# The start of a spectral layer: rows rounded from the raw row, statistics reordered

## The chip, the core and the metric

The kernel runs on one core of a Trainium2 chip. A core has TensorE (PE in the profile, with its weight loads as PEld), VectorE (DVE), ScalarE (ACT), GpSimd (POOL) and SyncE (SP), which here only issues transfers. Each engine works through its own queue in order, and an instruction that waits holds up what stands behind it. The metric is the device time of one execution in microseconds, the median of several runs.

## The reference

Four layers are applied to a sequence of 2048 rows of 576 numbers, alternately a Fourier mixing layer (A) and a gated long convolution (B), each on the normalized row and added to its input:

```python
def _layernorm(x, axis=-1, eps=1e-5):
    m = jnp.mean(x, axis=axis, keepdims=True)
    v = jnp.var(x, axis=axis, keepdims=True)
    return (x - m) / jnp.sqrt(v + eps)
...
a = jnp.einsum("bsd,ed->bse", x, dft_hid_re)
b = jnp.einsum("bsd,ed->bse", x, dft_hid_im)
y = jnp.einsum("ts,bse->bte", dft_seq_re, a) - jnp.einsum("ts,bse->bte", dft_seq_im, b)
...
x = x + _A_ref(_layernorm(x, axis=-1), ...)
x = x + _B_ref(_layernorm(x, axis=-1), B_k, B_v, B_shift_k, B_ssm_k, B_ssm_D)
x = x + _A_ref(_layernorm(x, axis=-1), ...)
x = x + _B_ref(_layernorm(x, axis=-1), B_k, B_v, B_shift_k, B_ssm_k, B_ssm_D)
```

B multiplies q by a causal convolution along the sequence of (short convolution of k, times v) with the kernel ssm_k, to which ssm_D adds at position 0. q is the normalized row; k, v, ssm_k, ssm_D are inputs, so all of the convolution can be computed beside the first A layer.

## The kernel before

**Numbers in two halves.** A float32 operand of a matmul is cut into a high half (rounded to the type float32r) and a low half (the value less the high half). `split` (lines 98 to 100) does so: ACT writes the high half, DVE subtracts it and writes the low half. A product takes three matmuls: high by high, high by low and low by high.

**Layer 1.** The 2048 positions are held as 16 "rows" of 128 partitions by 576 (the name row means such a block below). The sequence transform comes first. `layer` runs over steps (g, tb, k): g is the real or imaginary part, tb one of four blocks of 512 outputs, k one of 16 rows. A step loads one tile of `c_mat` (128 x 512), splits it (`load_c`; its halves lie in `mats`, written by L99 and L100), and multiplies row k by it: 12 matmuls into the banks `s0` to `s3` and two into `rm`, 14 in all. Step 0 is row 0 with tile 0, step 1 row 1 with tile 1, and so on.

**Making a row ready.** `load_x` issues a row's load into `early`. `norm_stats` takes its statistics: two half-row statistics (L183) and their joining (L184) on DVE, eps added (L185, DVE), the power -0.5 on POOL (L186). `normed` then forms the bias on DVE (L192) and scales the row in place on ACT (L193). `to_x` rounds the scaled row into `xs`, a part of `mats` (L197, ACT), and writes its low half with two subtractions on DVE (L199, L200). `get_x0` does this for row j, loads row j + 2 and takes row j + 1's statistics ahead.

**The branch.** `branch` is a generator that runs layer 2's convolution beside layer 1, one piece at each `next(br)`. In its first stage it loads rows of `ssm_k` ("kernel rows") and `v` with constants `f1c`, splits them (`f1_split`, into `f1r`), multiplies them (`f1_products`, banks `bf`), evacuates them on ACT (L453) and stores them. The first kernel row is row 1, then row 0, to whose first partition `ssm_D` is added (L431, DVE). The first constant is loaded through SP and rounded on ACT (L418), the others come by POOL's queue.

**The order of the work.** Within each engine a planner draws the order when the program is built; it takes what it holds to be ready, by need. `tc.issue_after(i)`, and `behind(i, j, ...)` for several, force that what is traced in the block on `i`'s engine stands behind `i` on that engine's queue; on other engines they do nothing, and they bring no wait. Lists keep the instructions to refer to: `parted` (the last split of the branch), `rounded`, `scaled`, `biased`, `pows`, `made` (a row's last subtraction), `halved` (the last tile's split), `stored` (the last evacuation of the branch), `anchor` (loads of c_mat).

**The beginning** (lines 769 to 787): row 0's load, 14 matmuls on zeros (`warm`), the first loads of the branch, row 0 made ready, the tiles 0 and 1 loaded and split, the loads of rows 1 and 2, then row 1 and two pieces of the branch. Then `layer` takes over.

Of the kernel before, what the change touches and what calls it, by code (L numbers as in the profile page):

```python
# [12 lines left out]
AF = mybir.ActivationFunctionType  # L13
OP = mybir.AluOpType
# [12 lines left out]
ASTAT = 8  # L27
XLEAD = 3
WARM = 14
EARLY = 6  # L30
ROWS = (0, 1, 2, 3, 4, 5, 6, 7, 8, 9)
K_FIRST = 4
# [34 lines left out]
def fnet_h3_kernel(ctx: ExitStack, tc: tile.TileContext, x, c_mat, w_re, w_im, k_pad, v, shift_k,  # L67
# [94 lines left out]

    anchor, made, rounded, pows, biased, halved, added, evac, parted, stored = [], [], [], [], [], [], [], [], [], []

    scaled = []

    def load_after(dst, src):
        with tc.issue_after(anchor[-1]):
            return nc.sync.dma_start(dst, src).ins
# [9 lines left out]
    def norm_stats(src):  # L179
        m = ring["stat"]()  # L180
        st, mv, ve, rs = m[:, :12].rearrange("p (a c) -> p a c", a=2), m[:, 12:14], m[:, 14:15], m[:, 15:16]
        for i in range(2):
            nc.vector.bn_stats(st[:, i, :], src[:, i * HD:(i + 1) * HD])  # L183
        nc.vector.bn_aggr(mv, st)  # L184
        nc.vector.tensor_scalar(ve, mv[:, 1:2], EPS, None, op0=OP.add)  # L185
        pows.append(nc.gpsimd.tensor_tensor(rs, ve, mhalf, OP.pow).ins)  # L186
        return mv, rs, m[:, 16:17]

    def normed(src, y):
        mv, rs, nb = norm_stats(src)  # L190
        yield
        biased.append(nc.vector.tensor_scalar(nb, mv[:, 0:1], rs, -1.0, op0=OP.mult, op1=OP.mult).ins)  # L192
        scaled.append(nc.scalar.activation(y, src, AF.Identity, bias=nb, scale=rs).ins)  # L193

    def to_x(y, j):
        t = xs[:, j, :]
        rounded.append(nc.scalar.activation(t[:, :D], y, AF.Copy).ins)  # L197
        h = t.bitcast(F32)
        nc.vector.tensor_tensor(t[:, D:D + REM], y[:, NC * P:], h[:, NC * P:D], OP.subtract)  # L199
        made.append(nc.vector.tensor_tensor(t[:, D + REM:], y[:, :NC * P], h[:, :NC * P], OP.subtract).ins)  # L200
        return t
# [10 lines left out]
    X = [None] * J  # L212
    CT = {}

    def load_c(step):
        g, tb, k = step
        raw = ring["craw"]()
        anchor.append(load_after(raw, c_mat[g, tb, k]) if anchor else nc.sync.dma_start(raw, c_mat[g, tb, k]).ins)
        c = ring["cs"]()
        t = c[:, :NT], c[:, NT:]  # L220
        with behind(*stored):
            halved[:] = split(t[0], t[1], raw)
        CT[step] = t
# [127 lines left out]
    def branch():  # L351
# [55 lines left out]
        def f1_loads(upto):  # L407
            while loads[0] < min(upto, len(todo)):
                j, src = todo[loads[0]]
                loads[0] += 1  # L410
                if j not in fcs:
                    fcs[j] = two(ring["fc"]())
                    if pows:
                        load_fr(fcs[j], f1c[j])
                    else:
                        raw = two(tmp[:, :2 * P])
                        nc.sync.dma_start(raw, f1c[j])
                        nc.scalar.activation(fcs[j], raw, AF.Copy)  # L418
                landed[j, src] = ring["land"]()
                nc.sync.dma_start(landed[j, src], (ssm_k if src else v)[:, j, :])  # L420
                if src and j == 0:
                    nc.sync.dma_start(tmp[:1, D:], ssm_d[None, :])

        def f1_split(j, src):
            r = landed.pop((j, src))
            if not src:
                row = rows[j // 2][:, j % 2, :]
                nc.vector.tensor_tensor(row, row, r, OP.mult)
                r = row
            elif j == 0:  # L430
                nc.vector.tensor_tensor(r[:1], r[:1], tmp[:1, D:], OP.add)  # L431
            if j < K_FIRST:
                xf = parts("xf")
                parted[:] = split(xf[0], xf[1], r)
                return xf
            if not src:
                t = ring["xp"]()
                paired[:] = t[:, :2 * D], t[:, 2 * D:]
            h, l = (t.rearrange("p (a s d) -> p a s d", a=2, s=2)[:, :, src, :] for t in paired)
            parted[:] = split(h, l, two(r))  # L440
            return tuple(paired)
# [15 lines left out]
        def visit(half):  # L457
            if visits and visits[0][0] <= half:
                f1_products(*visits.pop(0)[1:])

        for n, (j, src) in enumerate(todo):
            f1_loads(n + 1)
            if n < 2:
                yield
            xf = f1_split(j, src)
            if j < K_FIRST:
                visits += [(2 * n + 2, j, fcs[j], xf, hf * HD, HD, "so", hf * D + src * HD) for hf in range(2)]
            elif src:
                visits += [(2 * n + 3, j, fcs[j], xf, at, VW, "sp", at) for at in range(0, 2 * D, VW)]
            if n:  # L470
                f1_loads(n + 3)
            later = [m for m in range(n + 1, len(todo)) if todo[m][1] == 0 and 7 * (todo[m][0] // 2 + 1) > made_ops]
            for half in range(2):
                visit(2 * n + half)
                if later and n > 2:
                    left = 7 * (todo[later[0]][0] // 2 + 1) - made_ops
                    for _ in range(-(-left // (2 * (later[0] - n) - half)) if left > 0 else 0):
                        next(conv)
                        made_ops += 1
                yield  # L480
# [204 lines left out]
    def normed_x(src, y, junk):  # L685
        sm, rs, nb = sums(src, junk)
        yield
        nc.vector.tensor_tensor(nb, sm, rs, OP.mult)
        nc.scalar.activation(y, src, AF.Identity, bias=nb, scale=rs)
# [3 lines left out]
    def load_x(j):  # L693
        if j < J:
            XL[j] = ring["x"]()
            nc.sync.dma_start(XL[j], x[:, j, :])

    def stats0(j):
        if j < J and j not in LN:
            src = XL.pop(j)  # L700
            LN[j] = src, normed_x(src, src, ring["junk"]()) if j >= ASTAT else normed(src, src)
            next(LN[j][1])

    def get_x0(j):
        if X[j] is None:
            if j > 0:
                load_x(j + 2)
            stats0(j)
            if j > 0:
                with behind(*stored):  # L710
                    stats0(j + 1)
            src, ln = LN[j]
            with behind(*rounded[-1:]):
                next(ln, 0)
            X[j] = to_x(src, j)

    def done0(j, xa):
        nc.sync.dma_start(xa_d[j], xa)
# [50 lines left out]
    load_x(0)  # L769
    warm()  # L770
    next(br)
    get_x0(0)
    with tc.issue_after(biased[0]):
        next(br)
        with behind(*parted, scaled[0]):
            load_c((0, 0, 0))
        load_x(1)
        with behind(rounded[0]):
            load_c((0, 0, 1))
        load_x(2)  # L780
    used = 4
    first_lo = parted[1]
    next(br)
    next(br)
    with behind(first_lo):
        get_x0(1)
    next(br)
    next(br)
    spent = passed = 0.0
    total = (I2_END + 1 - MID_FROM) * STEP + 3 * 2 * TB * PIECE  # L790
# [384 lines left out]
```

## Time and profile before

| | us |
|---|---|
| median of 3 runs | 1185.11 |
| lowest, highest | 1184.79, 1185.26 |
| the profiled execution's own time | 1183.61 |
| its span, first to last instruction | 1181.8 |
| PE idle before its first matmul | 1.52 |
| ACT busy from 15 to 60 | 40.82 of 45 |
| DVE busy from 15 to 60 | 39.65 of 45 |

The mean granted TensorE clock is 0.999 of full speed. In the page's first part a row gives each engine's busy time, its share of the span and its instructions. A row of the windows gives a stretch and its length, then busy time and number of instructions for PE, PEld, DVE, ACT and POOL, the granted clock, the share of DMA engines busy and GB/s. A row of the waits says who waited for whom: us in all, times, longest. A row of the timeline gives start and length in us, the engine, the line, the operation, what it writes and reads, the shape and the number of instructions merged into the row; in brackets the idle time of the engine before it and what ended that. Matmuls and the passes of ACT and DVE overlap a little with the next one, so a start may lie before the end of the one before.

### The profile page before, as it was taken

The numbers are of one execution on the slowest core, as the hardware profiler recorded it, in microseconds if no ns is written. First come the engines' busy times: TensorE is split into PE (matmuls) and PEld (weight loads), VectorE is DVE, ScalarE is ACT, GpSimd is POOL, SyncE is SP. The second block draws the span as 40 slices with busy tenths as digits, with TensorE's granted clock in tenths as the row PEclk, the third lists the DMA queues.
The fourth block names the chain that finished last, engine by engine and source line by source line (L and its number), as shares of the span: only waits on it lengthen the run. The fifth ranks groups of instructions, "written<-read, shape, count | busy, mean of one in ns | idle before, by whom it ended". The sixth has DMA issues, their size and how long they took to land.

```text
span 1181.8 us, 18082 instructions
## 1 busy us (share of the span) xinstructions
PE 1167.8 (99%) x6198; PEld 989.1 (84%) x6198; DVE 868.6 (73%) x1564; ACT 650.8 (55%) x1280; POOL 75.5 (6%) x115
## 2 busy tenths in 40 slices
PE   8999999999999999999999999999999999999997
PEld 6776667988888888888888898888888888889997
DVE  7899983788877778787756765865776777774764
ACT  8865655577766667766645666534444445550210
POOL 2310000000000000001101111000000000001111
PEclk9999999999999999999999999999999999999999
DMA  9879898546666656648966777762872787894621
GB/s 336 284 232 316 263 300 272 160 152 173 213 214 193 203 168 193 190 140 247 270 192 215 249 240 231 247 253 73 257 249 72 221 284 258 260 338 144 219 93 40
DMA packets 147453, 255.64 MB, mean 216 GB/s; under 512 B 16161, under 2 KB 56353, under 8 KB 147362
## 3 DMA queue, kind: packets, MB, share of 16 engines
q1 hardware_dynamic: 111890, 210.17, 55.6%
q10 hardware_dynamic: 28560, 37.91, 9.2%
q0 software_dynamic: 6912, 6.43, 2.5%
q8 instruction: 48, 0.79, 0.3%
q14 instruction: 43, 0.35, 0.1%
HBM read 187.80 MB, written 66.65 MB: 215 GB/s over the span
## 4 chain that ended last, share of the span: by engine, by line
PE 77%; ACT 2%; DVE 2%; DMA 1%; issue 1%; ACTq 0%; DVEq 0%
PE s L76 43%; PE bk L76 30%; PE rm L76 4%; ACT flts L514 1%; ACT mid L514 1%; DVE mid L520 0%; DMA flts<-td 0%; DMA flts<-in_c_mat 0%; ACT mats L99 0%; DVE flts L534 0%; DVE flts L533 0%; DVE flts L532 0%; DVE flts L535 0%; ACTq L550 0%; ACT u L99 0%
## 5 line engine op out<-in xcount | busy, mean ns | idle before, releaser
L76 PE MATMUL s<-mats 128*128 128x512 f32 x2102 | 545.9, 395 | 4.2 <-ACT mats L197 2.4
L76 PEld LDWEIGHTS s<-mats 128*128 128x128 f32 x2102 | 382.7, 188 | 86.1 <-issue 10.9
L100 DVE TENSOR_TENSOR mats<-flts,mats 128x512 fp32r<-128x512 f32 x206 | 140.6, 686 | 50.3 <-ACT mats L99 48.9
L99 ACT ACTIVATE mats<-flts 128x512 fp32r<-128x512 f32 x206 | 128.2, 627 | 81.8 <-PE bk L76 30.7
L76 PE MATMUL bk<-mid 128*128 128x288 f32 x704 | 126.7, 300 | 2.1 <-DVE flts L289 0.8
L76 PEld LDWEIGHTS bk<-mid 128*128 128x128 f32 x704 | 108.6, 188 | 23.0 <-ACT flts L514 5.9
L514 ACT ACTIVATE flts<-bk 128x288 f32<-128x288 f32 (+1 forms) x192 | 76.5, 405 | 90.4 <-PE bk L76 71.6
L76 PE MATMUL bk<-w,u 128*128 128x288 f32 x864 | 120.6, 295 | 0.4 <-DVE w L243 0.4
L76 PEld LDWEIGHTS bk<-w,u 128*128 128x128 f32 x864 | 117.4, 188 | 3.5 <-ACT flts L514 0.9
L520 DVE TENSOR_TENSOR mid<-flts,mid 128x576 fp32r<-128x576 f32 (+1 forms) x149 | 93.3, 627 | 19.1 <-ACT mid L514 16.4
L76 PE MATMUL rm<-mats 128*128 128x512 f32 x304 | 94.5, 390 | 0.2 <-ACT flts L514 0.2
L514 ACT ACTIVATE mid<-flts 128x576 fp32r<-128x576 f32 (+1 forms) x148 | 80.5, 576 | 10.3 <-DVE flts L535 5.1
L289 DVE TENSOR_TENSOR flts<-flts,bk 128x288 f32<-128x288 f32 x48 | 21.8, 453 | 68.3 <-PE bk L76 65.9
L76 PE MATMUL bk<-mats 128*128 128x288 f32 (+1 forms) x376 | 67.8, 317 | 0.0
L76 PEld LDWEIGHTS rm<-mats 128*128 128x128 f32 x304 | 56.9, 188 | 12.6 <-ACT flts L514 0.6
L453 ACT ACTIVATE flts<-bf 128x384 f32<-128x384 f32 (+1 forms) x104 | 43.2, 462 | 43.4 <-PE bf L76 43.2
L76 PE MATMUL s<-t,mats 128*128 128x512 f32 x264 | 64.9, 389 | 0.0
L186 POOL TENSOR_TENSOR flts<-flts 128x1 f32<-128x1 f32 x34 | 28.0, 823 | 515.6 <-DVE flts L185 513.2
L76 PE MATMUL bk<-mats,t 128*128 128x288 f32 (+1 forms) x368 | 59.3, 303 | 0.0
L514 ACT ACTIVATE flts<-flts 64x288 f32<-64x288 f32 x128 | 56.6, 443 | 4.5
L76 PEld LDWEIGHTS bk<-mats 128*128 128x128 f32 x376 | 55.6, 188 | 3.4
L76 PEld LDWEIGHTS s<-t,mats 128*128 128x128 f32 x264 | 49.6, 188 | 10.3
(152 smaller groups left out, 1495.0 us busy)
## 6 DMA issues: line engine op xcount, KB each, us to landing
flts<-in_c_mat SPq DMA_DIRECT2D x148, 256.0 KB, 3.5
ph<-in_c_mat SPq DMA_DIRECT2D x54, 512.0 KB, 4.0
flts<-in_c_mat SPq DMA_DIRECT2D x30, 512.0 KB, 5.2
flts<-td SPq DMA_DIRECT2D x53, 288.0 KB, 3.1
td<-flts ACTq DMA_DIRECT2D x36, 384.0 KB, 4.2
vd<-flts ACTq DMA_DIRECT2D x64, 144.0 KB, 2.3
flts<-vd SPq DMA_DIRECT2D x32, 288.0 KB, 4.1
ud<-ph ACTq DMA_DIRECT2D x12, 512.0 KB, 6.7
```

The lines of the kernel that those rows point to most:

```text
L76: return nc.tensor.matmul(ps, lhsT, rhs, start=first, stop=last, skip_group_check=more).ins
L99: a = nc.scalar.activation(h, src, AF.Copy).ins
L100: return a, nc.vector.tensor_tensor(l, src, h.bitcast(F32), OP.subtract).ins
L186: pows.append(nc.gpsimd.tensor_tensor(rs, ve, mhalf, OP.pow).ins)
L289: added[:] = [nc.vector.tensor_tensor(r[:, cs], r[:, cs], ps[:, :HD], OP.add).ins]
L453: stored[:] = [nc.scalar.activation(so[:, i, :], ps[i], AF.Copy).ins]
L514: last_act.append(nc.scalar.activation(*args, **kw).ins)
L520: nc.vector.tensor_tensor(l, src, h.bitcast(F32), OP.subtract)
```

## The change

Rows 0 and 1 (`DIRECT`) get their high half in one activation from the raw row, with the same scale and bias as the scaling; the scaling follows for the low half. The start is traced in another order: row 0's bias, rounding and scaling; tile 0 behind the rounding; the loads on SP in the order tile 0, x row 1, tile 1, x row 2; row 1's statistics in full (`stats0(1)`), and row 0's low half behind them; row 1; the piece of the branch with the first product and kernel row 0's split; tile 1's split with its low half behind row 0's; row 2's statistics behind row 1's bias and tile 1's low half; the second product. The statistics of rows 3 and 4 stand behind the variance of the row before. Kernel row 0's `ssm_D` is added on POOL instead of DVE, behind row 1's power; its split stands on ACT behind the first product's evacuation and row 1's rounding, kernel row 2's behind row 1's rounding.

```diff
+DIRECT = 2
...
-    scaled = []
+    scaled, varied, led = [], [], []
...
-        nc.vector.tensor_scalar(ve, mv[:, 1:2], EPS, None, op0=OP.add)
+        varied.append(nc.vector.tensor_scalar(ve, mv[:, 1:2], EPS, None, op0=OP.add).ins)
...
-    def normed(src, y):
+    def normed(src, y, h=None):
         mv, rs, nb = norm_stats(src)
         yield
         biased.append(nc.vector.tensor_scalar(nb, mv[:, 0:1], rs, -1.0, op0=OP.mult, op1=OP.mult).ins)
+        if h is not None:
+            rounded.append(nc.scalar.activation(h, src, AF.Identity, bias=nb, scale=rs).ins)
         scaled.append(nc.scalar.activation(y, src, AF.Identity, bias=nb, scale=rs).ins)
 
-    def to_x(y, j):
+    def to_x(y, j, direct=False):
         t = xs[:, j, :]
-        rounded.append(nc.scalar.activation(t[:, :D], y, AF.Copy).ins)
+        if not direct:
+            rounded.append(nc.scalar.activation(t[:, :D], y, AF.Copy).ins)
...
-    def load_c(step):
+    def raw_step(step):
         g, tb, k = step
         raw = ring["craw"]()
         anchor.append(load_after(raw, c_mat[g, tb, k]) if anchor else nc.sync.dma_start(raw, c_mat[g, tb, k]).ins)
+        return raw
+
+    def load_c(step, raw=None):
+        raw = raw_step(step) if raw is None else raw
...
+                landed[j, src] = ring["land"]()
+                led.append(nc.sync.dma_start(landed[j, src], (ssm_k if src else v)[:, j, :]).ins)
                 if j not in fcs:
...
-                        nc.sync.dma_start(raw, f1c[j])
+                        with behind(*led):
+                            led.append(nc.sync.dma_start(raw, f1c[j]).ins)
                         nc.scalar.activation(fcs[j], raw, AF.Copy)
-                landed[j, src] = ring["land"]()
-                nc.sync.dma_start(landed[j, src], (ssm_k if src else v)[:, j, :])
...
-                nc.vector.tensor_tensor(r[:1], r[:1], tmp[:1, D:], OP.add)
+                nc.gpsimd.tensor_tensor(r[:1], r[:1], tmp[:1, D:], OP.add)
...
-            xf = f1_split(j, src)
+            if n == 1:
+                visit(2)
+            with behind(*(stored + pows[1:2] + rounded[1:2] if n == 1 else rounded[1:2] if n == 2 else ())):
+                xf = f1_split(j, src)
...
-                visit(2 * n + half)
+                if n != 1 or half:
+                    visit(2 * n + half)
...
     def load_x(j):
         if j < J:
             XL[j] = ring["x"]()
-            nc.sync.dma_start(XL[j], x[:, j, :])
+            led.append(nc.sync.dma_start(XL[j], x[:, j, :]).ins)
 
     def stats0(j):
         if j < J and j not in LN:
             src = XL.pop(j)
-            LN[j] = src, normed_x(src, src, ring["junk"]()) if j >= ASTAT else normed(src, src)
+            if j >= ASTAT:
+                LN[j] = src, normed_x(src, src, ring["junk"]())
+            else:
+                LN[j] = src, normed(src, src, xs[:, j, :D] if j < DIRECT else None)
             next(LN[j][1])
 
     def get_x0(j):
         if X[j] is None:
-            if j > 0:
+            with behind(*led[-1:] if j < DIRECT else ()):
                 load_x(j + 2)
             stats0(j)
-            if j > 0:
-                with behind(*stored):
+            src, ln = LN[j]
+            if j > 1:
+                with behind(*stored, *varied[j:j + 1] if j < K_FIRST else ()):
                     stats0(j + 1)
-            src, ln = LN[j]
             with behind(*rounded[-1:]):
                 next(ln, 0)
-            X[j] = to_x(src, j)
+            X[j] = to_x(src, j, j < DIRECT)
...
-    get_x0(0)
+    stats0(0)
+    next(LN[0][1], 0)
     with tc.issue_after(biased[0]):
         next(br)
-        with behind(*parted, scaled[0]):
+        with behind(*parted, rounded[0], *led):
             load_c((0, 0, 0))
-        load_x(1)
-        with behind(rounded[0]):
-            load_c((0, 0, 1))
-        load_x(2)
+        with behind(anchor[-1]):
+            load_x(1)
+        with behind(led[-1]):
+            raw = raw_step((0, 0, 1))
+        with behind(anchor[-1]):
+            load_x(2)
     used = 4
     first_lo = parted[1]
     next(br)
     next(br)
     with behind(first_lo):
-        get_x0(1)
+        stats0(1)
+    with behind(varied[1]):
+        X[0] = to_x(LN[0][0], 0, True)
+    get_x0(1)
     next(br)
+    with behind(made[0]):
+        load_c((0, 0, 1), raw)
+    with behind(biased[1], halved[1]):
+        stats0(2)
     next(br)
```

## The prediction

> **What bounds the kernel now.** I read the head of the page first, then the busy time in windows, then the waits of the first 15 us, and last the order in time of each engine.
>
> ```profile
> span 1181.8 us, 18082 instructions
> PE 1167.8 (99%) x6198; PEld 989.1 (84%) x6198; DVE 868.6 (73%) x1564; ACT 650.8 (55%) x1280; POOL 75.5 (6%) x115
> ```
>
> ```profile
> 15.00:60.00 45.00, 45.00 (x216) 34.59 (x215) 39.65 (x96) 40.82 (x84) 11.85 (x12) 1.00 0.85 304
> 60.00:1175.00 1115.00, 1111.67 (x5943) 946.98 (x5941) 815.93 (x1430) 599.83 (x1180) 58.62 (x93) 1.00 0.67 213
> ```
>
> TensorE (PE) is busy for 99% of the span, without a gap from 15 to 60 us, and idle for 1115 - 1111.67 = 3.33 us in the next 1115. What PE gains at the start is therefore carried to the end, unless ACT, DVE or a load can't follow. What it can gain is in the waits before 15 us:
>
> ```profile
> PE s L76 <- ACT mats L197: 2.4, 2, 1.4
> PE s L76 <- DVE mats L761: 1.5, 1, 1.5
> PE s L76 <- DVE mats L100: 0.2, 1, 0.2
> ```
>
> The 1.5 us are for the warm-up's tile, which the change leaves alone. The rest, 2.4 + 0.2 us, are waits for rows 0 and 1 of layer 1. PE's order in time:
>
> ```profile
> 6.49 0.66 PE L76 MATMUL bf<-f1r 64*128 64x288 f32 x6
> 8.17 0.73 PE L76 MATMUL s<-mats 128*128 128x512 f32 x2 [1.02 <-ACT mats L197]
> 9.09 0.73 PE L76 MATMUL s<-mats 128*128 128x512 f32 x2 [0.18 <-DVE mats L100]
> 9.75 0.66 PE L76 MATMUL bf<-f1r 64*128 64x288 f32 x6
> 10.34 2.11 PE L76 MATMUL s<-mats 128*128 128x512 f32 x8
> 12.29 0.63 PE L76 MATMUL rm<-mats 128*128 128x512 f32 x2
> 14.30 3.03 PE L76 MATMUL s<-mats 128*128 128x512 f32 x12 [1.38 <-ACT mats L197]
> 17.63 2.92 PE L76 MATMUL s<-mats 128*128 128x512 f32 x12
> 20.93 0.67 PE L76 MATMUL bf<-f1r 64*128 64x288 f32 x6
> 21.52 3.05 PE L76 MATMUL s<-mats 128*128 128x512 f32 x12
> ```
>
> Step 0 (row 0 against c_mat's tile 0) runs from 8.17, steps 1, 2 and 3 begin at 14.30, 17.63 and 21.52; a product of the branch (bf) lies inside step 0. A step with its two rm takes 17.63 - 14.30 = 3.33 us, about 0.23 a matmul, so step 0's last slot ends at 12.29 + 2 x 0.23 = 12.75, and step 1 could have begun there: 1.55 us are lost (the bracket's 1.38 counts from the drain of the last matmul).
>
> What PE waits for stands on ACT:
>
> ```profile
> 5.84 0.42 ACT L418 ACTIVATE f1r<-f1f 128x256 fp32r<-128x256 f32 x1 [0.80 <-DMA f1f<-in_f1c]
> 6.17 0.85 ACT L193 ACTIVATE early<-early,flts 128x576 f32<-128x576 f32 x1
> 6.93 0.61 ACT L99 ACTIVATE mats<-flts 128x512 fp32r<-128x512 f32 x1
> 7.45 0.67 ACT L197 ACTIVATE mats<-early 128x576 fp32r<-128x576 f32 x1
> 8.64 0.63 ACT L99 ACTIVATE mats<-flts 128x512 fp32r<-128x512 f32 x1 [0.52 <-DMA flts<-in_c_mat]
> 9.18 0.69 ACT L453 ACTIVATE flts<-bf 128x288 f32<-128x288 f32 x2
> 10.34 0.69 ACT L99 ACTIVATE f1r<-flts 128x576 fp32r<-128x576 f32 x1 [0.47 <-DMA flts<-in_ssm_k]
> 12.23 0.87 ACT L193 ACTIVATE early<-early,flts 128x576 f32<-128x576 f32 x1 [0.42 <-DVE flts L192]
> 13.01 0.67 ACT L99 ACTIVATE f1r<-flts 128x576 fp32r<-128x576 f32 x1
> 13.58 0.67 ACT L197 ACTIVATE mats<-early 128x576 fp32r<-128x576 f32 x1
> 15.96 0.67 ACT L197 ACTIVATE mats<-early 128x576 fp32r<-128x576 f32 x1
> 18.14 0.67 ACT L197 ACTIVATE mats<-early 128x576 fp32r<-128x576 f32 x1
> ```
>
> Each row is scaled (L193), then rounded (L197): row 0 at 6.17 and 7.45, row 1 at 12.23 and 13.58, rows 2 and 3 rounded at 15.96 and 18.14. Row 1's scaling waits 0.42 us for its bias (DVE L192), and kernel row 0's split (13.01) stands between its two passes. Row 1's statistics on DVE and POOL show why the bias is late:
>
> ```profile
> 7.26 1.18 DVE L183 BATCH_NORM_STATS2 flts<-early 128x6 f32<-128x288 f32 x3 [0.92 <-DMA early<-in_x]
> 8.36 0.67 DVE L100 TENSOR_TENSOR mats<-flts,mats 128x512 fp32r<-128x512 f32 x1
> 8.95 0.22 DVE L199 TENSOR_TENSOR mats<-early,mats 128x64 fp32r<-128x64 f32 x1
> 9.09 0.69 DVE L200 TENSOR_TENSOR mats<-early,mats 128x512 fp32r<-128x512 f32 x1
> 10.29 0.20 DVE L184 BATCH_NORM_AGGREGATE flts<-flts 128x2 f32<-128x12 f32 x1
> 10.73 0.14 DVE L185 TENSOR_SCALAR flts<-flts 128x1 f32<-128x1 f32 x1
> 10.79 0.73 DVE L431 TENSOR_TENSOR flts<-flts,f1f 1x576 f32<-1x576 f32 x1
> 11.99 0.21 DVE L192 TENSOR_SCALAR flts<-flts 128x1 f32<-128x1 f32 x1 [0.35 <-POOL flts L186]
> ```
>
> ```profile
> 10.96 0.99 POOL L186 TENSOR_TENSOR flts<-flts 128x1 f32<-128x1 f32 x1 [4.89 <-DVE flts L185]
> 12.34 0.55 POOL L186 TENSOR_TENSOR flts<-flts 128x1 f32<-128x1 f32 x1 [0.39 <-DVE flts L185]
> 41.38 4.20 POOL L655 TENSOR_TENSOR flts<-flts 128x1 f32<-128x1 f32 x1 [2.99 <-DVE flts L654]
> ```
>
> Row 1's halves are done by 8.08, but they are joined (L184) only at 10.29, behind both tiles' low halves and row 0's. Its power on POOL then takes 0.99 us where another takes 0.55: it ended at 11.95, 0.43 after DVE's L431 (11.52).
>
> **Part 1: row 0 rounded from the raw row.** The new activation has L193's operands and only another destination, so I price it 0.85; it takes the scaling's place at 6.17, behind L418. The tile's high half stays at 6.93 to 7.54, and the scaling, now needed for the low half alone, follows. PE began 0.05 after the rounding's end (8.12), so now at 7.60: -0.57. The other bound: the planner puts the scaling ahead of tile 0, 0.75 later, and PE begins at 8.35: +0.18. I take the first, because in the old order too tile 0 went ahead of the pass that depends on the one before.
>
> **Part 2: tile 0's low half.** Row 2's statistic leaves DVE's place ahead of it (0.36), and row 1's joining (0.20 and 0.14, with starts of 0.03) may come in: it ends between 8.67 and 9.10 instead of 9.03. I take 9.10. PE is there earlier and meets the wait for longer: old, two matmuls and 0.36 of lost slots; new, four high matmuls to about 8.55 and some 0.50: +0.14. Ends: 0 lost if the second bf product fits in (its bank's evacuation now stands ahead of tile 1), 0.94 if two matmuls alone go first, so -0.36 to +0.58. Step 0 ends at 12.75 - 0.57 + 0.14 = 12.32.
>
> **Part 3: row 1.** Row 1's variance is ready at 8.5 to 9.1. The power then meets DVE's tile-0 low half and row 0's L199 and L200, which end at 9.10 + 0.22 + 0.69, less overlaps, 9.84; as with L431 it ends 0.43 later, 10.27 (9.1 if nothing blocked it). Bias 0.21 and its hand-over: 10.50; rounding 0.87: 11.4, against 14.25 before. Step 0 ends at 12.32, so 0.9 us of slack hides the rest, and the 1.55 go: -1.55. If that cover is gone, each further 0.1 of the power costs 0.1. Tile 1's high half now stands behind the first product's evacuation, about 8.9 to 9.5; its low half, behind row 0's, ends about 11.0; both are hidden by step 0. Row 1's scaling follows to 12.2 and its low half to 13.1; before, that was done at 15.40, 1.1 after the step's start, and nothing waited; now it has till 13.4.
>
> SP issues tile 1 ahead of x row 2: their landings, 0.7 us apart (between 7.26 and 8.64 two came), change places. Row 2 is not read before 11, so this is hidden.
>
> **Part 4: kernel row 0.** Its add (0.73 on DVE) goes to POOL behind row 1's power, its split behind row 1's rounding. Its product is the next bf on PE, at 20.93, which covers it. Wide work on POOL is nowhere in the trace; bounds: 0.55, POOL's shortest, and 0.55 + 0.73 = 1.28. I take the high end. Behind it in POOL's queue stand two constant loads and row 2's power.
>
> **Part 5: row 2.** Its statistics now wait for row 1's bias and tile 1's low half: 11.0, then 0.81 + 0.20 + 0.14 to 12.2, a power that row 1's low half holds to 13.1 + 0.43 = 13.5, bias 13.75, two dependent passes 0.86 and 0.67 to 15.35. ACT also has an evacuation, two splits and tile 2 to place there, some 0.6 each; I take one, 15.9, where before the rounding ended at 16.63, 1.0 ahead of need. Step 1 ends at 12.32 + 3.33 = 15.65: a new wait, +0.30 (ends: 0 and 1.6). Row 3 had 21.52 - 18.81 = 2.7 us of slack, which covers it and those after.
>
> **The sum:** -0.57 + 0.14 - 1.55 + 0.30 = -1.68: step 2 at 15.95. The profiled execution took 1183.61, 1.50 below the median of 1185.11; 1181.9 by it, 1183.4 as a median.
>
> **Rivals.**
> A. The whole start is hidden: the product fills the wait for tile 0, row 2 is in time, step 2 at 7.60 + (4.58 - 0.36) + 3.33 = 15.15, -2.5, and a little of the later 3.33 goes too: 1182.4. For it: ACT had 0.52 + 0.47 + 0.42 us idle before row 2, and three later rows' statistics leave DVE. Against: row 2's are put back as well.
> B. POOL's add begins before tile 1's low half and holds DVE: 10.27 + 1.28 + 0.68 = 12.2 instead of 11.0, row 2's rounding 1.1 later at 16.4, step 2 at 16.5, -1.1: 1184.0. For it: 10.96 shows the pair excluding each other; against: DVE's own add there was not held. The Trainium skill, SBUF — State Buffer, Who interferes with whom, says that a VectorE instruction with two SBUF inputs and a GpSimd one that reads SBUF exclude each other for the whole instruction, whichever began first; the 0.43 us behind L431 agrees.
> C. Slower: POOL starves. At 41.38 one power took 4.20, 3.65 too long, while DVE ran two-input work back to back. Row 2's power stands behind the add; if both starve so, the rounding comes 7.3 later, 22.65 against the old start of 17.63: +5.0, 1190.1. It decides from 4.6 us of delay on (0.2% slower). Against: DVE's queue soon waits for that bias itself and falls idle.
> D. The planner draws later orders anew from the shifted start and leaves 4 us of idle beside today's 3.33: 1187.6. Against: nothing is edited there.
>
> **How the numbers follow.** Forecast 0.34, its own range 1182.6 to 1184.9 from the bounds; A 0.30, B 0.20, C 0.09, D 0.07. 0.2%, about what a measurement of this kernel tells from no change, is 2.4 us. A and 0.02 of the forecast lie beyond it: faster 0.32; C and D: slower 0.16; the rest 0.52. The range reaches below A for 0.6 of later gains and up to 1187.0, leaving out C, D and tails.
>
> **What would show it.** Rounding of row 0 ending at 7.0 and PE's first s at 7.60; a wait of about 0.5 for tile 0's low half; no wait ahead of step 1, begun near 12.3; step 2 near 15.95, perhaps after a short wait for row 2's rounding; POOL's add under 1.3. A step 2 after 17.6, or PE idle of over 5 us between 60 and 1175, would make the prediction wrong.

## The result, and the profile after

The changed kernel takes 1187.66 us (median of 10 runs, 1186.82 to 1188.62) beside 1183.90 for the kernel before on the same chip (1181.90 to 1185.26): ratio 1.0031, 95% interval 1.0023 to 1.0039. It is slower by 3.8 us, where 1.7 us less was forecast. Its profiled execution took 1188.62 us. First the head of the page and the busy time in windows of the changed kernel (columns as before):

```profile
span 1186.8 us, 18091 instructions
PE 1169.9 (99%) x6198; PEld 989.6 (83%) x6198; DVE 870.0 (73%) x1563; ACT 651.4 (55%) x1280; POOL 75.3 (6%) x116
```

```profile
15.00:60.00 45.00, 42.06 (x197) 31.26 (x198) 38.43 (x97) 40.11 (x82) 10.54 (x12) 1.00 0.90 321
60.00:1175.00 1115.00, 1110.14 (x5918) 944.46 (x5917) 816.83 (x1431) 601.64 (x1182) 58.69 (x93) 1.00 0.67 212
```

PE's idle time from 15 to 60 us has gone from nothing to 45 - 42.06 = 2.94 us, and after 60 from 3.33 to 4.86. The timeline of PE shows where:

```profile
1.52 5.57 PE L77 MATMUL s<-mats 128*128 128x512 f32 x14 [1.52 <-DVE mats L777]
7.02 0.67 PE L77 MATMUL bf<-f1r 64*128 64x288 f32 x6
7.61 1.76 PE L77 MATMUL s<-mats 128*128 128x512 f32 x5
...
12.08 1.98 PE L77 MATMUL s<-mats 128*128 128x512 f32 x8
15.35 1.21 PE L77 MATMUL s<-mats 128*128 128x512 f32 x4 [1.29 <-DVE mats L204]
...
18.09 3.03 PE L77 MATMUL s<-mats 128*128 128x512 f32 x12 [1.07 <-ACT mats L201]
...
53.72 2.11 PE L77 MATMUL s<-mats 128*128 128x512 f32 x8 [0.67 <-DVE mats L101]
...
56.78 2.06 PE L77 MATMUL s<-mats 128*128 128x512 f32 x6 [0.72 <-ACT mats L201]
...
81.43 0.66 PE L77 MATMUL bf<-f1r 64*128 64x288 f32 x6 [0.43 <-ACT flts L462]
...
97.71 0.80 PE L77 MATMUL bf<-f1r 64*128 64x384 f32 x6 [1.01 <-ACT flts L462]
```

Step 0 begins 0.56 us earlier (8.17 - 7.61), step 1 2.22 earlier (14.30 - 12.08). Then step 1 stands 1.29 us for row 1's low half, step 2 1.07 us for row 2's rounding, and it begins at 18.09, 0.46 later than before. The lower four waits, 2.8 us in all, are in places that the diff does not edit.

The offset of a layer step, below, is the start of its first matmul less that in the profile of before. It is +0.58 us from step 3 to step 11, +2.43 at step 12 and +3.73 at step 28, and stays there to 209 us. So in this execution 0.6 us were lost at the start, instead of 1.7 won, and 3.15 between steps 4 and 28. (A wait costs more than its bracket, which counts from the drain of the last matmul: the two between steps 11 and 12 add up to 1.39 us and cost 1.85.)

Why row 1's low half is late stands on DVE, ACT and POOL (timelines of the changed kernel):

```profile
10.23 1.78 DVE L101 TENSOR_TENSOR mats<-flts,mats 128x512 fp32r<-128x512 f32 x1
11.94 0.81 DVE L184 BATCH_NORM_STATS2 flts<-early 128x6 f32<-128x288 f32 x2
...
13.09 0.81 DVE L184 BATCH_NORM_STATS2 flts<-early 128x6 f32<-128x288 f32 x2
13.82 0.74 DVE L101 TENSOR_TENSOR f1r<-flts,f1r 128x576 fp32r<-128x576 f32 x1
...
14.61 0.69 DVE L204 TENSOR_TENSOR mats<-early,mats 128x512 fp32r<-128x512 f32 x1
...
39.96 0.15 DVE L667 TENSOR_SCALAR flts<-flts 128x1 f32<-128x1 f32 x1 [0.74 <-ACT early L666]
40.78 0.16 DVE L701 TENSOR_TENSOR flts<-flts 128x1 f32<-128x1 f32 x1 [0.66 <-POOL flts L668]
41.48 0.15 DVE L667 TENSOR_SCALAR flts<-flts 128x1 f32<-128x1 f32 x1 [0.54 <-ACT early L666]
42.29 0.16 DVE L701 TENSOR_TENSOR flts<-flts 128x1 f32<-128x1 f32 x1 [0.66 <-POOL flts L668]
...
52.99 0.68 DVE L101 TENSOR_TENSOR mats<-flts,mats 128x512 fp32r<-128x512 f32 x1
```

```profile
5.82 0.87 ACT L195 ACTIVATE mats<-early,flts 128x576 fp32r<-128x576 f32 x1
6.60 0.61 ACT L100 ACTIVATE mats<-flts 128x512 fp32r<-128x512 f32 x1
...
10.35 0.87 ACT L195 ACTIVATE mats<-early,flts 128x576 fp32r<-128x576 f32 x1 [1.27 <-DVE flts L193]
11.49 0.69 ACT L100 ACTIVATE f1r<-flts 128x576 fp32r<-128x576 f32 x1 [0.27 <-POOL flts L440]
12.08 0.85 ACT L196 ACTIVATE early<-early,flts 128x576 f32<-128x576 f32 x1
...
14.94 0.63 ACT L100 ACTIVATE mats<-flts 128x512 fp32r<-128x512 f32 x1 [0.89 <-DMA flts<-in_c_mat]
15.53 0.87 ACT L196 ACTIVATE early<-early,flts 128x576 f32<-128x576 f32 x1
16.84 0.63 ACT L100 ACTIVATE mats<-flts 128x512 fp32r<-128x512 f32 x1 [0.44 <-PE rm L77]
17.37 0.67 ACT L201 ACTIVATE mats<-early 128x576 fp32r<-128x576 f32 x1
```

```profile
8.99 1.07 POOL L187 TENSOR_TENSOR flts<-flts 128x1 f32<-128x1 f32 x1 [2.81 <-DVE flts L186]
10.04 1.42 POOL L440 TENSOR_TENSOR flts<-flts,f1f 1x576 f32<-1x576 f32 x1
...
13.26 0.56 POOL L187 TENSOR_TENSOR flts<-flts 128x1 f32<-128x1 f32 x1 [0.71 <-DVE flts L186]
```

Row 1 is rounded by 11.22, where 11.4 was forecast. But tile 1's low half, begun 0.19 us after POOL's add (10.04 to 11.46), takes 1.78 us instead of 0.68, kernel row 0's split stands between row 1's two passes on ACT, and row 2's and row 3's statistics and kernel row 0's low half stand ahead of row 1's low half on DVE. For row 2, ACT has tiles 3 and 4 ahead of its passes: one waits for its load, the other for its slot.

Between 39 and 43 us DVE idles for 0.74 + 0.66 + 0.54 + 0.66 = 2.60 us, taking the statistics of rows 10 and 11 one after the other; the kernel before did branch products there. They come later instead, and tile 11's low half ends at 53.67. This is how tightly the kernel before had it (timelines of DVE and of PE of the kernel before; the first row of PE is the warm-up):

```profile
39.89 1.35 DVE L400 TENSOR_TENSOR f1f<-f1f 128x1152 f32<-128x1152 f32 x1
...
50.37 0.69 DVE L100 TENSOR_TENSOR mats<-flts,mats 128x512 fp32r<-128x512 f32 x1
```

```profile
1.52 5.00 PE L76 MATMUL s<-mats 128*128 128x512 f32 x14 [1.52 <-DVE mats L761]
...
51.06 3.00 PE L76 MATMUL s<-mats 128*128 128x512 f32 x12
...
54.36 1.72 PE L76 MATMUL s<-mats 128*128 128x512 f32 x6
```

Its tile 11's low half ended at 51.06, when step 11 began, and the step's second matmul reads it, at 51.40: PE had no gap, and some 0.3 us of slack.

### The profile page after: what moved, and what is told of

Read it like the earlier page. It is cut to its first block, busy times and chain, and to the rows that moved or that the text cites. A ratio compares the mean times of both kernels' runs of the same rounds, so it can differ in the third digit from the quotient of the medians.

```text
span 1186.8 us, 18091 instructions
## 1 busy us (share of the span) xinstructions
PE 1169.9 (99%) x6198; PEld 989.6 (83%) x6198; DVE 870.0 (73%) x1563; ACT 651.4 (55%) x1280; POOL 75.3 (6%) x116
## 4 chain that ended last, share of the span: by engine, by line
PE 75%; ACT 2%; DMA 2%; DVE 2%; issue 1%; ACTq 0%; SPq 0%; DVEq 0%
PE s L77 41%; PE bk L77 30%; PE rm L77 4%; ACT flts L527 1%; ACT mid L527 1%; DMA flts<-in_c_mat 1%; ACT mats L100 0%; DMA ph<-in_c_mat 0%; DMA flts<-td 0%; DMA gate<-xa 0%; DVE mid L533 0%; DVE flts L547 0%; ACT gate L702 0%; DVE flts L546 0%; DMA y<-gate 0%
```

## The experiments

Offsets in us, each from one profiled execution; times are medians, the kernel before in parentheses. By the instruction order of each queue, read in the programs, two orders stand from about 20 us on: b, that of before, and c, that of the changed kernel. Before 20 us they differ with the edits; after 105 us on PE, and after 150 on every queue, all agree but e15 and e16 (to 206 us) and e17 and e18 (to 727).

An offset at the start is also a matter of the execution. The changed kernel, e8, e10 and e14 have the same queues up to 20 us, and their step 2 lies at +0.46, +0.12, +0.58 and +1.79: in e14 row 1's statistics had to wait for its load until 8.54 us, in the changed kernel until 7.18. Among e7, e9, e13, e15 and e17, alike up to 17 us, it lies between -1.95 and -1.33. What is lost after step 4 depends less on this: 3.15 us in the changed kernel, 2.91 in e10 with its order.

| kernel | order | step 2 | step 4 | step 12 | step 28 | time | ratio, 95% interval |
|---|---|---|---|---|---|---|---|
| changed | c | +0.46 | +0.58 | +2.43 | +3.73 | 1187.66 (1183.90) | 1.0031, 1.0023-1.0039 |
| e1_no_add | near c | +2.28 | +5.21 | +6.28 | +7.41 | 1191.58 (1184.56) | 1.0057, 1.0039-1.0074 |
| e2_low1_first | near b | -1.17 | +0.07 | +0.89 | +1.06 | 1186.01 (1184.56) | 1.0011, 1.0002-1.0021 |
| e3_direct_only | c | -0.35 | -0.16 | +1.79 | +2.78 | 1186.72 (1184.56) | 1.0020, 1.0011-1.0029 |
| e4_warm32 | c | +2.25 | +2.22 | +4.06 | +4.46 | 1188.33 (1184.56) | 1.0031, 1.0020-1.0042 |
| e5_warm28 | b | +0.87 | +0.84 | +0.84 | +0.87 | 1185.55 (1184.95) | 1.0011, 1.0001-1.0020 |
| e6_stats_behind_row1 | near b | +0.37 | +1.48 | +2.27 | +2.47 | 1187.40 (1184.95) | 1.0020, 1.0011-1.0028 |
| e7_add_on_dve | near b | -1.95 | -1.44 | +0.05 | +0.24 | 1186.02 (1184.95) | 1.0010, 1.0001-1.0018 |
| e8_third_order | own | +0.12 | +0.22 | +2.38 | +3.05 | 1188.17 (1184.95) | 1.0031, 1.0019-1.0043 |
| e9_row12_root | near b | -1.74 | -1.24 | +0.33 | +0.49 | 1185.95 (1184.93) | 1.0012, 1.0004-1.0021 |
| e10_after_row12_root | c | +0.58 | +0.68 | +2.59 | +3.59 | 1188.03 (1184.93) | 1.0032, 1.0019-1.0045 |
| e11_before_row12_root | b to 50 us | +0.35 | +0.33 | +0.31 | +0.72 | 1186.02 (1184.93) | 1.0011, 1.0002-1.0019 |
| e12_rows8_root | own | +0.17 | +0.44 | +3.47 | +3.24 | 1187.76 (1184.93) | 1.0023, 1.0014-1.0031 |
| e13_less_conv | own | -1.45 | -0.95 | -0.95 | +1.13 | 1186.76 (1184.83) | 1.0019, 1.0010-1.0028 |
| e14_after_less_conv | own | +1.79 | +1.89 | +1.89 | +3.58 | 1187.94 (1184.83) | 1.0023, 1.0014-1.0032 |
| e15_branch_later | own | -1.33 | -0.84 | -0.84 | +4.33 | 1189.29 (1184.83) | 1.0033, 1.0020-1.0045 |
| e16_before_branch_later | own | +0.44 | +0.43 | +0.51 | +4.06 | 1189.29 (1184.83) | 1.0031, 1.0020-1.0041 |
| e17_mean_on_act | own | -1.58 | -1.07 | +5.51 | +6.03 | 1191.53 (1185.63) | 1.0050, 1.0037-1.0062 |
| e18_before_mean_on_act | near b | -0.23 | -0.24 | -0.26 | -0.60 | 1186.60 (1185.63) | 1.0009, 1.0000-1.0017 |

### Parts of the start, and PE later (e1 to e4)

```
e1:  -  nc.gpsimd.tensor_tensor(r[:1], r[:1], tmp[:1, D:], OP.add)
e2:  kernel row 0's split also behind scaled[1] and made[1]; rows 3, 4's statistics behind made[1]
e3:  before.py with rows 0 and 1 rounded from the raw row, tile 0 behind that rounding; nothing else of the change
e4:  before.py with WARM = 32
```

> The changed kernel without the addition of ssm_D to kernel row 0 (on neither engine; the output lacks that term). Theory 1 (POOL's add makes row 1's low half and row 2 late, by holding DVE during tile 1's low half, 1.78 us instead of 0.68, and by holding up kernel row 0's split, which stands ahead of row 1's second pass): tile 1's low half takes 0.7, row 1's low half is written by 14.0 instead of 15.3, step 2 begins at 17.0 or earlier instead of 18.09, and the span falls by 1 us or more. Theory 2 (the order on ACT and DVE does it, whoever adds): tile 1's low half is quick, but row 1's low half still ends after 14.6 and step 2 begins at 17.6 or later. Either way the time from step 3 to 105 us is the planner's and may fall out differently by 1 to 2 us.

> The changed kernel with kernel row 0's split behind row 1's second pass on ACT and behind row 1's low half on DVE, and the statistics of rows 3 and 4 behind row 1's low half too; the add stays on POOL. Theory 2 (order): row 1's second pass begins at 11.2 instead of 12.08, its low half ends by 14.0, PE's wait of 1.29 in step 1 goes or falls under 0.4, step 2 begins at 17.2 or earlier. Theory 1 (the add): tile 1's low half still takes 1.8, row 2's statistics still begin at 11.9, and step 2 begins at 17.6 or later although step 1 has no wait.

> The kernel before with nothing changed but rows 0 and 1 rounded from the raw row (tile 0 behind that rounding). If this part works as its row was priced: step 0 at 7.60 instead of 8.17, row 1 rounded at 13.1 instead of 14.25 (it takes the scaling's place), step 1 at 13.2 instead of 14.30, step 2 limited by row 2's rounding at 16.6 and so at 16.7 to 17.0 instead of 17.63, -0.6 to -0.9. Theory 3 (the order from 20 to 105 us is drawn anew at every change and costs or saves 1 to 4 us of its own): the span moves by over 1 us against the offset at step 3. Without theory 3: the span is that of the kernel before less 0.6 to 0.9.

> The kernel before with 32 instead of 14 matmuls on zeros at the start: the order on every queue stays as it was, PE alone comes later. 18 matmuls of 0.23 us put step 0 at about 10.7 and step 1 at 14.7 to 15.0; the offset at step 2 is +0.4 to +0.8, as large as the changed kernel's +0.46. If the changed kernel's later loss (offset +0.6 at 51 us, +2.8 at 58, +4.3 at 105) comes from the late start alone, it shows here too. If it comes from the order that was drawn anew (theory 3), the offset stays within 0.3 of that at step 2 up to 190 us, and the median is 0.3 to 1.0 above before.

In e1 the output lacks ssm_D. It confirms one thing and misses the rest. Without the add, tile 1's low half takes 0.68 us again (DVE timeline of e1):

```profile
10.54 0.68 DVE L101 TENSOR_TENSOR mats<-flts,mats 128x512 fp32r<-128x512 f32 x1
```

But the order drawn without the add puts the next kernel row's split ahead of row 2's scaling on ACT, where it stands 2.79 us for its load (ACT and PE timelines of e1):

```profile
17.32 0.68 ACT L100 ACTIVATE f1r<-flts 128x576 fp32r<-128x576 f32 x1 [2.79 <-DMA flts<-in_ssm_k]
```

```profile
19.91 5.49 PE L77 MATMUL s<-mats 128*128 128x512 f32 x12 [2.51 <-ACT mats L201]
```

e2 brings step 2 to 16.46 with the add left on POOL. It does not part the order from the add, as it was meant to: under its order the add began at 10.47, after tile 1's low half (10.08), which took 0.68 us again. e3 is the telling one: a start that is 0.16 us early at step 4, with the smallest part of the change, ends 2.78 late. e4 was no pure shift, as its expectation had it: its queues have order c, step 2 lies at +2.25 instead of +0.4 to +0.8, and the offset grew by 2.24 after step 4.

### The order alone (e5, e6, e8)

```
e5:  before.py with WARM = 28
e6:  -  with behind(*stored, *varied[j:j + 1] if j < K_FIRST else ()):
     +  with behind(*stored, *varied[j:j + 1] + made[1:2] if j < K_FIRST else ()):
e8:  the same edge list with  *(made[5:6] if j == 6 else ())  added
```

> The kernel before with WARM = 28 instead of 14: fourteen more zero products on TensorE ahead of step 0, nothing else; every other queue has exactly the order of the kernel before (with 32, run e4_warm32, the queues have the changed kernel's order between about 20 and 105 us). Theory 1 (the time is lost by the order drawn for 20 to 105 us, not by where step 0 stands): step 1 late by 1.0 to 1.6 us, and that offset is the same or smaller at step 28; time 1185.0 to 1186.3. Rival (any shift of the start runs into transfers and waits later and grows by itself): the offset grows from step 11 to step 28 by 2 us or more as it did with 32, time about 1188.

> The changed kernel with one more edge: the statistics of rows 3 and 4 also wait for row 1's low half. With it the queues from step 4 on fall back nearly to the order of the kernel before. Theory 1 (order): steps 2 to 4 gain 0.2 to 1.0 us by row 1's low half coming earlier, and from step 4 to step 28 the offset grows by at most 1.2 us instead of 3.2; time 1185.0 to 1186.5. Rival (the loss comes from the start itself, POOL's add and the split of kernel row 0, which stay as they are): growth of 3 us as in the changed kernel, time 1187 to 1188.

> The changed kernel with one more edge, the statistics of row 6 behind row 5's low half. Every queue keeps the changed kernel's order up to step 4 or 5; from there to about 105 us a third order results, different from both kernels'. Theory 1a (the changed kernel's order is a particularly poor draw, above all through row 12's power and tile 11): the growth from step 4 to step 28 differs clearly from 3.15 us, most likely smaller, 0 to 2.5; time 1185 to 1187. Theory 1b (every order but that of before costs about the same, since the kernel before was fitted to its own): growth 2.2 to 3.2 as in the four kernels that have the changed order; time 1187 to 1188. Rival (the start itself): offset at step 4 as in the changed kernel, +0.58, and growth 3.15.

e4 and e5 differ in four products of zeros. DVE of e5 goes on with a branch product where DVE of e4 idles (timelines of e5, then of e4):

```profile
40.73 1.35 DVE L400 TENSOR_TENSOR f1f<-f1f 128x1152 f32<-128x1152 f32 x1
```

```profile
41.60 0.15 DVE L654 TENSOR_SCALAR flts<-flts 128x1 f32<-128x1 f32 x1 [1.48 <-ACT early L653]
42.42 0.16 DVE L688 TENSOR_TENSOR flts<-flts 128x1 f32<-128x1 f32 x1 [0.66 <-POOL flts L655]
```

From step 4 to step 28 e5's offset grows by 0.03 us, e4's by 2.24. e4's shift is larger, 2.22 us at step 4 against e5's 0.84, but the changed kernel's is smaller, 0.58, and e3 starts early, and both lose some 3 us under order c. That settles where most of the loss comes from: not from the shift, but from the order drawn after it. (e5's profiled execution lost 5 us more after 1029 us, which its median does not show.) e6, one edge away from the changed kernel, grows by 0.99 instead of 3.15, though its start is worse: PE waits 2.61 us in step 1, as DVE stood 1.81 us for a row's load. e8's edge, which holds back row 7's statistics (not row 6's, as its expectation says), gives a third order, and that costs 2.83.

### A good start, and what becomes of it (e7, e9 to e12)

```
e7:  -  nc.gpsimd.tensor_tensor(r[:1], ...)   +  nc.vector.tensor_tensor(r[:1], ...)
     and kernel row 0's split also behind made[1]
e9:  e7, row 12:  -  nc.gpsimd.tensor_tensor(rs, sv, mhalf, OP.pow)
                  +  nc.scalar.activation(sv, sv, AF.Sqrt); nc.vector.reciprocal(rs, sv)
e10, e11: the same in after.py and before.py;  e12: e7 with it for rows 8 to 15
```

> The changed kernel with the add of ssm_D back on DVE and kernel row 0's split held behind row 1's low half, so that no long POOL operation stands beside tile 1's low half; the queues from step 4 on are nearly in the order of the kernel before. Theory of the start (POOL's add holds DVE, and work for kernel row 0 and row 3 queued ahead of row 1's low half costs the wait in step 1): tile 1's low half takes 0.68 us and ends at 10.8 to 11.2, row 2's power on POOL starts by 12.3 instead of 13.26, row 1's low half ends at 14.1 or before instead of 15.30, step 2 starts at 16.2 to 16.7 (before 17.63, changed kernel 18.09); time 1184.5 to 1186.0. Rival (step 2 is held by another thing, such as row 2's load or tile 2): step 2 stays at 17.5 or later.

> Run e7_add_on_dve with row 12's power taken off POOL: a square root on ACT and a reciprocal on DVE in its place; the order of the queues is otherwise that of e7. Theory (step 12 loses the start's gain because row 12's power stands on POOL for 3.60 us behind DVE's run of two-input operations): row 12 is rounded before 53.9 us, step 12 follows step 11 without its wait of 0.47, the offset at step 12 is -1.0 to -0.6 instead of +0.05 and at step 28 -0.8 to -0.3 instead of +0.24; time 1184.5 to 1185.6. Rival (DVE is simply full there, 10.00 of 10 us between 40 and 50, so what follows the power is late whoever computes it): row 12 rounded at 54.2 or later, step 12 still waits, offset 0.0 to +0.3, time as e7.

> The changed kernel with row 12's power as a square root on ACT and a reciprocal on DVE, nothing else; the queues keep the changed kernel's order. Theory (row 12's power, 4.13 us on POOL, is one cause of the loss at steps 12 and 13): the waits of 0.72 and 0.13 us at 56.8 and 58.1 us go, the wait of 0.67 for tile 11's low half stays; offset at step 12 +1.2 to +1.8 instead of +2.43, at step 28 +2.2 to +3.1 instead of +3.73; time 1186.3 to 1187.2. Rival (DVE full): offsets as in the changed kernel.

> The kernel before with row 12's power as a square root on ACT and a reciprocal on DVE. There it took 1.59 us and row 12 was rounded 0.25 us ahead of step 12, so nothing is gained: offsets at steps 4 to 28 within 0.2 us of zero, time 1184.4 to 1185.4. If the time falls by 1 us or more, POOL's powers cost the kernel elsewhere and the control fails.

> Run e7_add_on_dve with the powers of rows 8 to 15 all as a square root on ACT and a reciprocal on DVE. It removes every long power between 34 and 62 us, but the queues then get an order of their own from about 35 us on. If the power's wait is what matters, step 12 starts at 53.9 or before and step 28 stands at -1.4 to 0; if any order that differs from that of before costs 1 to 3 us there, the offset at step 28 is above +0.5 although no power is held any more. Time 1183.8 to 1185.5 by the first, 1186 to 1187.5 by the second.

e7's start is the one that was forecast for the change; it puts right the add and the order at once, so that no run says how much each of the two cost. Timelines of PE and of DVE of e7:

```profile
12.19 2.96 PE L77 MATMUL s<-mats 128*128 128x512 f32 x12
...
15.68 3.42 PE L77 MATMUL s<-mats 128*128 128x512 f32 x12
...
51.35 2.12 PE L77 MATMUL s<-mats 128*128 128x512 f32 x8 [0.46 <-DVE mats L101]
...
54.41 1.91 PE L77 MATMUL s<-mats 128*128 128x512 f32 x6 [0.47 <-ACT mats L201]
```

```profile
9.89 0.68 DVE L101 TENSOR_TENSOR mats<-flts,mats 128x512 fp32r<-128x512 f32 x1
...
12.99 0.69 DVE L204 TENSOR_TENSOR mats<-early,mats 128x512 fp32r<-128x512 f32 x1
13.59 0.74 DVE L440 TENSOR_TENSOR flts<-flts,f1f 1x576 f32<-1x576 f32 x1
```

Step 1 has no wait, step 2 begins at 15.68, 1.95 us early, and 1.44 us are left at step 4. All of it is gone at step 12, in the same two waits as in the changed kernel: tile 11's low half and row 12. Row 12's power took 3.60 us on POOL there, so I took it off. That theory fell: in e9 the reciprocal was done 2.1 us earlier (49.57 against 51.71), row 12 was rounded no earlier, and e10 kept its waits too. (e11, the same edit on the kernel before, has +0.72 at step 28, where at most 0.2 was expected.) Timeline of ACT in e9:

```profile
51.67 0.78 ACT L666 ACTIVATE early<-early,flts 128x576 f32<-128x576 f32 x1 [0.82 <-DVE flts L665]
...
53.96 0.67 ACT L201 ACTIVATE mats<-early 128x576 fp32r<-128x576 f32 x1
```

Row 13's second pass stands ahead of row 12's scaling on ACT and waits for a mean (L665) queued on DVE behind branch products; DVE is full, 10.00 of 10 us from 40 to 50. e12, whose queues were drawn anew from 13 us on, lost 2.8 us after step 4 with no power on POOL for these rows.

### The amount of DVE's work, and attempts at a faster version (e13 to e18)

```
e13, e14: e7 and after.py; the branch's 7th and 9th operation on DVE cut to 64 of 576 columns
e15, e16: e7 and before.py;  -  F1_16 = 5   +  F1_16 = 4
e17, e18: e7 and before.py; the mean's factor on ACT
     -  nc.scalar.activation(junk, src, AF.Copy, accum_out=sm)
     -  nc.vector.tensor_scalar(sm, sm, -1.0 / D, None, op0=OP.mult)
     +  nc.scalar.activation(junk, src, AF.Copy, scale=-1.0 / D, accum_out=sm)
```

> Run e7_add_on_dve with two of the branch's products on DVE (its seventh and ninth, 1.35 us each) cut to 64 of 576 columns, so that part of the branch's result is not computed; DVE has some 2.4 us less to do between 40 and 50 us. Theory A (DVE's amount of work there is the bound): the offset at step 12, +0.05 in e7, falls to -1.5 to -0.8 and stays below -0.5 at step 28; time 1183.8 to 1185.0. Theory B (the order alone): offset at step 12 above -0.3, some other wait in place of the two; time 1185.5 to 1187.

> The changed kernel with the same two products cut to 64 columns (part of the branch's result is not computed). Theory A: the waits of 0.67 and 0.72 us ahead of the products at 53.7 and 56.8 us fall to 0.2 or less; offset at step 12 +0.6 to +1.4 instead of +2.43, at step 28 +1.2 to +2.6 instead of +3.73; time 1185.5 to 1186.8. Theory B: offset at step 28 above +3; time 1187 to 1188.

> Run e7_add_on_dve with F1_16 = 4 instead of 5: up to step 16 the branch does one step in four steps' time less, and catches up by step 42. Nothing is left out. Theory A: step 12 starts at -1.5 to -1.0, the waits at steps 11 and 12 are gone; what is put off costs as much PE time later, so that the time is 1183.5 to 1185.0, ahead of the kernel before by up to 1.4 us. Theory B: a redrawn order brings waits of its own of 1 to 3 us; time 1185.5 to 1188.

> The kernel before with F1_16 = 4. It has no wait on TensorE between 45 and 100 us, so that there is nothing to win: by theory A the time stays within 0.5 us of before, 1184.4 to 1185.4; by theory B the redrawn order costs 1 to 3 us, 1186 to 1188.

> Run e7_add_on_dve with the mean's factor -1/D given to ACT's first pass, so that its sum comes out as minus the mean and the operation on DVE between the two passes (L665, 0.15 us, with the way there and back) falls away for all rows from 8 on and in the later layers; the queues are drawn anew. Theory (ACT's stand of 0.8 us for a mean queued on DVE behind the branch's work keeps row 12 late): ACT has no wait for a mean between 46 and 56 us, step 12 starts at -1.5 to -0.7, offset at step 28 below 0; time 1183.0 to 1184.8. Rival (a redrawn order brings another wait of 1 to 3 us): offset at step 28 above +0.8, time 1185.5 to 1188.

> The kernel before with the same edit of the mean. TensorE has no wait there between 18 and 105 us, so by the theory nothing is gained at steps 4 to 28 (offsets within 0.3 us of zero) and the time is 1184.3 to 1185.4; by the rival the redrawn order costs 1 to 3 us, offset at step 28 above +0.8, time 1185.8 to 1188.

In e13 and e14 a part of the branch's result is not computed. With 2.1 us less on DVE (two operations of 0.28 us instead of 1.35), both waits at steps 11 and 12 are gone, from the good start (e13: -0.95 from step 3 to 12) and from the changed one (e14: +1.89 throughout). That speaks for DVE's load as the cause of these two waits, but it is not shown alone: from 41 us on the orders of DVE and ACT in both runs also differ from those of e7 and of the changed kernel. Yet e13 loses 2.08 and e14 1.69 us after that, to tile 15's low half and to the branch's evictions on ACT: other waits took their place. e15 and e16 put branch work off and lost 5.2 and 3.6 us after step 4. e17 lost 7.1: an eviction drawn ahead of row 12's work on ACT stood for a store's landing (ACT timeline of e17):

```profile
48.76 0.41 ACT L462 ACTIVATE flts<-bf 128x288 f32<-128x288 f32 x1 [5.64 <-DMA td<-flts]
```

Behind PE's longest waits in e15, e16 and e17 the granted clock fell to one half (last section), which is a part of what these three lost. e18, the same edit on the kernel before, kept PE's order nearly as it was and lost nothing (-0.36). Over all kernels, the offset grew from step 4 to step 28 by -0.4 to 1.7 us in order b or near it, by 2.2 to 3.2 in c or near it, and by 1.7 to 7.1 in others. No version was faster than the kernel before. The five kernels within 0.9 us of it at step 28 (e5, e7, e9, e11, e18) measure 0.6 to 1.1 us slower, up to 1.6 more than their offsets say. In e7's profiled execution 0.9 us of this came where layer 2 begins (offset 0.24 at 209 us, 1.10 at 216) and 0.6 after 260 us; why stays open.

## Why the prediction was wrong

- Part 1's number, step 0 at 7.60, was hit (7.61) by luck. Row 0 was rounded by 6.69 and tile 0's high half by 7.21, 0.33 earlier than forecast, but PE came late: the 14 matmuls of the warm-up, which the change leaves alone, took 5.57 us instead of 5.00 (they follow each other after 0.43 us at first and after 0.23 later, and the pace changed at about 6.0 us instead of 4.8), and the branch's product stood between. Part 2 nearly held: tile 0's low half ended at 8.59 without a wait for it, where one of about 0.5 was forecast, and step 1 began at 12.08 (12.32).
- Part 3 held up to row 1's rounding, 11.22 (11.4), and the 1.55 us were won. Its last sentences are the step at which the forecast of the start failed: "Row 1's scaling follows to 12.2 and its low half to 13.1" came at 12.93 and 15.30. I gave that half till 13.4 without asking what the planner puts ahead of it on two engines.
- Part 4: the add took 1.42 us, above my bound of 1.28. "Its product is the next bf on PE, at 20.93, which covers it" is true of the product, but not of the split, which held up row 1 on ACT and on DVE.
- Rival B's mechanism came as priced up to tile 1's low half, which took 1.78 us and ended at 12.01, against 12.2. The Trainium skill, SBUF — State Buffer, Who interferes with whom, states this lock, and the 1.78 us agree (1.77 in e14); without the add the operation took 0.68 in e1. B's step 2, 16.5, did not come, for B left the orders on ACT and DVE as the forecast had them. Nor did rival C: row 2's power took 0.56 us.
- Part 5: row 2 was rounded at 18.04, not 15.9. The price of "an evacuation, two splits and tile 2" was taken as durations; two of the passes waited, 0.89 and 0.44 us, and the bias itself came at 15.5 behind row 1's low half. Step 2 at 18.09 lies past the 17.6 that was named as refuting it. With the add and the two orders put right (e7) step 2 stood at 15.68, where the sum had 15.95.
- The larger error is the price of rival D, "The planner draws later orders anew from the shifted start", given 0.07 because "nothing is edited there". This happened in the changed kernel, in e3 and in e4, and cost 3.15, 2.94 and 2.24 us between steps 4 and 28. Its time, 1187.6 beside 1187.66, fits by luck: it put 4 us of idle time beside the 3.33 after 60 us, where 4.86 were measured, 1.53 more; the rest was lost before 60 us, at the start and at steps 11 and 12.
- The premise under it was the first paragraph's "What PE gains at the start is therefore carried to the end, unless ACT, DVE or a load can't follow". Under the orders that were drawn they could not: e7's 1.44 us did not pass step 12.

Not settled: how the loss at the start divides between the add and the two orders; which of the planner's estimates tips it from order b to c (four products of zeros do), and whether a start could keep its gain under exactly order b; no kernel with an earlier start had it.

## What to carry to other kernels

Where a planner draws the order at build time, an edit at the start changes the order far behind it. Compare the queues of both programs all along before pricing the edited lines, and shift the start by itself as a control. A PE without gaps is no sign of slack: look how early its operands end. In a queue that runs in order, price what stands ahead of the instruction that is needed, and what each of those waits for.

## What the runs showed of the hardware

A wait on PE can cost more than its length. In e1 the 12 matmuls behind the wait of 2.51 us took 5.49 us instead of some 3.0. The windows of e1 show a granted clock (third number from the end) of one half, which lasted to about 26 us:

```profile
16.00:18.00 2.00, 1.40 (x6) 0.68 (x4) 2.00 (x10) 0.68 (x2) 0.55 (x1) 1.00 1.06 415
19.90:22.00 2.10, 2.09 (x5) 1.71 (x6) 2.03 (x7) 2.07 (x3) 0.84 (x1) 0.50 0.93 320
```

The same came in e15 after a wait of 2.02 us, in e16 after 2.40, in e17 after 2.63 and in e5 after 2.75 (at 1034 us), but not in e6 after one of 2.61. In e5 and e9 it also came at 214 and 213 us, where the longest wait just before had been 1.33 and 1.27 us. So the length of one wait does not decide it in these runs. The Trainium skill, TensorE: Matmul & The Clock Gate, Why this matters for your kernels, warns of gaps of more than about 3 us; here shorter ones did it.

POOL's add of 1x576 took 1.42 us, and 1.58 in e2, against 0.74 on DVE in e7. One-input statistics on DVE beside it in e2 kept their 0.45 us each (two in 0.82):

```profile
10.68 0.82 DVE L184 BATCH_NORM_STATS2 flts<-early 128x6 f32<-128x288 f32 x2
```
